# Threshold attention and GELU MLP on one core: order of the first loads, place and pace of the MLP, and a fifth pair with PE transposes

## The chip, the cores and the metric

The kernel runs on one core of a Trainium2 chip. The core has a matrix engine (TensorE, PE in the profile; PEld is its weight load), a vector engine (VectorE, DVE), an activation engine (ScalarE, ACT), GpSimd (POOL) and a queue engine (SyncE, SP). Each works through its own program in order, and they wait for each other on semaphores. The metric is the device time of one execution in microseconds (us), smaller is better; a kernel counts as faster or slower when its time differs by more than 2%.

## The reference

Attention on 8 batches of 8 heads (576 tokens, head size 64) in which only scores within `tau` of the row's maximum count, and after it an MLP with exact GELU on all 4608 tokens. The weights `w_in` and `w_out` come as 64-bit floats.

```python
# q, k, v: (8, 8, 576, 64) float32; tau = 0.02
scores = scale * np.matmul(q, k.transpose(0, 1, 3, 2))
thresh = np.max(scores, axis=-1, keepdims=True) - tau
scores = np.where(scores >= thresh, scores, -1000000000.0)
scores = scores - np.max(scores, axis=-1, keepdims=True)
attn = np.exp(scores)
attn = attn / (np.sum(attn, axis=-1, keepdims=True) + 1e-09)
attn_out = np.matmul(attn, v)
# bridge: (B,H,S,D) -> (B*S, H*D), x: (4608, 512)
h = x @ w_in                                   # (512, 2048)
g = 0.5 * h * (1.0 + erf(h * inv_sqrt2))
return g @ w_out                               # (2048, 512)
```

## The kernel before

The unit of attention is a pair of heads: 4 pairs in each batch, 32 in all. A pair has 5 slots: four of 128 query rows for both heads, and a last one for the 64 remaining rows of both heads. Slots of the first four pairs are walked in two sweeps, rows 0 to 255 of all four pairs first, so that a first block of x is there early. The MLP works on blocks of 256 tokens, 18 in all, and is laid between the slots in single steps.

At the start the loads are issued, and the first transposes:

```python
    load_early(0)
    for _ in range(4):
        load_piece()
    load_early(1)
    turn_qk_early(0)
    load_early(2)
```

A weight piece (512 columns of 128 rows) is loaded twice by GpSimd, once shifted by three bytes, and put together to 32-bit floats by three operations of VectorE, one of ScalarE and one more of VectorE:

```python
            piece = None
            if raws:
                dst, raw, shifted = raws.pop(0)
                hi = raw.rearrange("p (f w) -> p f w", w=2)[:, :, 1]
                top = shifted.rearrange("p (f w) -> p f w", w=2)[:, :, 0]
                expo, power = (gp.tile([P, PIECE], U32, tag="g", name=s) for s in ("expo", "power"))
                vec.tensor_scalar(expo, hi, 0x7FF00000, None, op0=ALU.bitwise_and)
                nc.scalar.activation(power, expo, AF.Relu, bias=rebias, scale=8.0)
                piece = dst, hi, top, power
                yield 340
            if ahead:
                dst, hi, top, power = ahead
                mant = gp.tile([P, PIECE], U32, tag="g", name="mant")
                vec.tensor_scalar(mant, top, 0x0FFFFFFF, 0x10000000, op0=ALU.bitwise_and, op1=ALU.bitwise_or)
                yield 340
                vec.scalar_tensor_tensor(power, hi, 0x80000000, power, op0=ALU.bitwise_and, op1=ALU.bitwise_or)
                yield 720
                vec.scalar_tensor_tensor(dst, mant, 2.0 ** -28, power.bitcast(FP32), op0=ALU.mult, op1=ALU.mult)
                load_piece()
                converted[0] += 1
                yield 700
            ahead = piece
```

The first four pairs ("early") turn q, k and the probabilities with PE, against the identity or a diagonal that holds the reciprocal of the row sum, so that the turn also scales. The others scale with VectorE, turn blocks of 32 x 32 with VectorE, and regroup them by DMA:

```python
    def softmax_tail(p, i, early):

        s = st[p]
        sc, thr, w = s.pop(("sc", i)), s.pop(("thr", i)), s["p", i]
        n = len(sc)
        den = small.tile([P, 2], FP32, tag="den", name="den")
        for e in range(n):
            row = w[:, e * S:(e + 1) * S].rearrange("p (h s) -> p h s", h=2)
            nc.vector.scalar_tensor_tensor(
                row, sc[e][:, :, 0:HALF], thr[:, e:e + 1], row, op0=ALU.is_ge, op1=ALU.mult,
                accum_out=den[:, e:e + 1])
        rden = small.tile([P, 2], FP32, tag="rden", name="rden")
        nc.vector.tensor_scalar(den[:, 0:n], den[:, 0:n], 1e-9, None, op0=ALU.add)
        nc.vector.reciprocal(rden[:, 0:n], den[:, 0:n])
        if early:
            diag = s["diag", i] = dg.tile([P, 2, P], FP32, tag="diag", name="diag")
            for e in range(n):
                nc.scalar.activation(diag[:, e, :], ident, AF.Copy, bias=0.0, scale=rden[:, e:e + 1])
            return
        for e in range(n):
            row = w[:, e * S:(e + 1) * S]
            nc.vector.tensor_scalar(row, row, rden[:, e:e + 1], None, op0=ALU.mult)

        s = st[p]
        w = s.pop(("p", i))
        n = 1 if i == NC else 2
        for e in range(n):
            to = pd_tail[p % 2] if i == NC else pd[e][:, :, i * Q:(i + 1) * Q]
            nc.vector.transpose(to[:, 0:NB, :], w[:, e * S:(e + 1) * S].rearrange("p (b i) -> p b i", i=Q))
        if i == NC - 1:
            s["pT"] = [one.tile([P, KR, S], FP32, tag=f"pT{e}", name=f"pT{e}") for e in range(2)]
            for e in range(2):
                for a in range(4):
                    regroup(s["pT"][e], a * P, P, pd[e], a)
        if i == NC:
            for a in range(4):
                e, at = divmod(a * Q, TAIL)
                regroup(s["pT"][e], MAIN + at, Q, pd_tail[p % 2], a)
# ...
    def turn_p_early(p, i):


        s = st[p]
        if i == 0 or (p < HP and i == 2):
            s["pT"] = [one.tile([P, KR, S], FP32, tag=f"pT{e}", name=f"pT{e}") for e in range(2)]
        w, diag = s.pop(("p", i)), s.pop(("diag", i))
        n = 1 if i == NC else 2

        def turn(to, cols, e):
            nc.tensor.matmul(to, lhsT=w[:, cols], rhs=diag[:, e, :], start=True, stop=True)

        for e in range(n):
            tr = ps.tile([P, NC, P], FP32, tag="mm", name="tr")
            for c in range(NC):
                at = e * (S + TAIL) + c * P
                turn(tr[:, c, :], slice(at, at + P), e)
            if i < NC:
                nc.scalar.copy(s["pT"][e][:, 0:NC, i * P:(i + 1) * P], tr)
```

The scores of a slot need two PSUM buffers of the tag `sc`, and there are two, so scores of the next slot wait until `softmax_tail` of this one has read them (L360).

The loop over slots, with the pace of the MLP:

```python
    BATCH = HP * SLOTS
    WEIGH = 2
    START = 2 * HP + 1

    goal = [0.55] + [1.85 + 2.06 * i for i in range(B - 1)]


    PART = (1.0, 1.2, 1.0, 1.0, 0.8)

    tokens = 0
    owed = 0.0
    for n in range(len(slots) + WEIGH + 1):
        p, i = slots[n] if n < len(slots) else divmod(n, SLOTS)
        batch = n // BATCH
        early = p < EARLY
        last = slots[n - 1] if 0 < n <= len(slots) else None
        if p < NP:
            scores(p, i)
            softmax_head(p, i)
        if last and last[0] < EARLY:
            turn_p_early(*last)
        if p < NP:
            softmax_tail(p, i, early)
            if not early and i:
                for c in range(0 if i == 1 else i, i + 1):
                    turn_p(p, c)
        if p < HP - 1 and i == 0:
            turn_qk_early(p + 1)
            if p == 0:
                load_early(3)
        if p < HP and i == NC and 0 < p < HP - 1:
            load(p + 3)
        if n == BATCH:
            convert(1e12)
            for t in pd_tail:
                nc.gpsimd.memset(t[:, NB:4 * KR, :], 0.0)
        if p >= HP and i == 1 and p + 2 < NP:
            load(p + 2)
        if p >= HP - 1 and i == 2 and p + 1 < NP:
            turn_qk(p + 1)
        convert(3000 if n < 2 * HP else 3600)
        if n >= START:
            done = min(batch, B - 1)
            rest = BATCH if done else BATCH - START
            part = PART[i] if not early and batch < B else 1.0
            owed += part * (goal[done] - (goal[done - 1] if done else 0.0)) * BLK_NS / rest
            if n % 2 or n >= EARLY * SLOTS:
                fill(owed, tokens)
                owed = 0.0
# ...
        if p > EARLY and i == WEIGH:
            for h in range(2):
                weigh_v(p - 1, h * HALF, (h + 1) * HALF)
            if p % HP == 0:
                tokens = p // HP * S
    convert(1e12)
    fill(1e12, B * S)
```

`goal` says how many blocks of the MLP should be issued by the end of each batch of 20 slots; `fill` issues steps until the debt is paid, and stops when the next block's x is not there (`tokens`) or its weights are not converted.

## Time and profile before

| | before |
|---|---|
| time, median of 3 (lowest, highest) | 1504.81 us (1501.78, 1504.85) |
| span of the profiled execution | 1498.2 us |
| mean granted clock of PE | 0.990 |
| matmuls of the MLP (L436, L447), busy | 516.7 + 515.7 us |
| matmuls of scores (L335) | 161.9 + 35.4 us |
| matmuls with v (L408) | 168.4 us |
| turns of early probabilities on PE (L281) | 47.4 us |
| weights moved by GpSimd's queue | 33.54 MB |

The profile page has a line of busy times for each engine, a strip of 40 equal slices of the span with the busy share in tenths, the DMA queues, the chain of work that ended last, and the costliest groups of instructions. A group's row gives line, engine and operation, what is written from what, the shape, the count, busy us and mean ns of one, and the idle time of the engine just before, with what ended it. Besides the page, the trace can be asked for waits, for a timeline, and for the busy time by windows. Times in a timeline row are start and length in us; square brackets hold the idle time before it and what released it.

### The profile page before, as it was taken

The numbers are of one execution on the slowest core, as the hardware profiler recorded it, in microseconds if no ns is written. First come the engines' busy times: TensorE is split into PE (matmuls) and PEld (weight loads), VectorE is DVE, ScalarE is ACT, GpSimd is POOL, SyncE is SP. The second block draws the span as 40 slices with busy tenths as digits, with TensorE's granted clock in tenths as the row PEclk, the third lists the DMA queues.
The fourth block names the chain that finished last, engine by engine and source line by source line (L and its number), as shares of the span: only waits on it lengthen the run. The fifth ranks groups of instructions, "written<-read, shape, count | busy, mean of one in ns | idle before, by whom it ended". The sixth has DMA issues, their size and how long they took to land.

```text
span 1498.2 us, 17694 instructions
## 1 busy us (share of the span) xinstructions
PE 1434.2 (96%) x6288; PEld 904.9 (60%) x6288; DVE 928.9 (62%) x2125; ACT 595.0 (40%) x886; POOL 41.2 (3%) x86
## 2 busy tenths in 40 slices
PE   3888899989999999989999999999999999999998
PEld 2566546546564747465656566666656565765764
DVE  3997788886667577766777677767767776100000
ACT  3657526535352525234444444444435352210110
POOL 2222100000000000000000000000000000000000
PEclk9999999999999999999999999999999999999999
DMA  7877336655555625463555554454544534300000
GB/s 230 245 242 239 109 76 128 115 121 105 103 104 106 117 64 101 95 135 64 110 106 111 99 111 98 105 98 98 103 95 97 106 73 94 79 14 8 7 14 14
DMA packets 390823, 155.05 MB, mean 103 GB/s; under 512 B 229456, under 2 KB 379984, under 8 KB 390736
## 3 DMA queue, kind: packets, MB, share of 16 engines
q1 hardware_dynamic: 383568, 120.38, 39.7%
q0 software_dynamic: 7168, 33.54, 6.5%
q8 instruction: 51, 0.84, 0.2%
q14 instruction: 36, 0.29, 0.1%
HBM read 61.85 MB, written 9.44 MB: 48 GB/s over the span
## 4 chain that ended last, share of the span: by engine, by line
PE 81%; DVE 11%; DMA 3%; SPq 2%; ACT 2%; issue 1%; DVEq 0%; ACTq 0%
PE o_ps L447 31%; PE hT L436 30%; PE sc L335 10%; PE xT L408 9%; DVE p L360 3%; DVE nmx L346 2%; SPq L397 2%; DMA pT<-pd 1%; DVE pd L385 1%; DMA q<-in_q_dram 1%; DVE power L176 1%; DVE expo L167 1%; DVE w_in L178 1%; PE tr L281 1%; ACT p L347 1%
## 5 line engine op out<-in xcount | busy, mean ns | idle before, releaser
L436 PE MATMUL hT<-x,w_in 128*128 128x256 f32 x2304 | 516.7, 382 | 0.7 <-ACT pT L289 0.7
L447 PE MATMUL o_ps<-w_out,g 128*128 128x512 f32 x1152 | 515.7, 598 | 0.0
L436 PEld LDWEIGHTS hT<-x,w_in 128*128 128x128 f32 x2304 | 433.1, 190 | 83.9 <-issue 26.1
L447 PEld LDWEIGHTS o_ps<-w_out,g 128*128 128x128 f32 x1152 | 214.4, 190 | 258.3 <-issue 254.7
L346 DVE TENSOR_REDUCE nmx<-sc 128x1 f32<-128x576 f32 x288 | 205.6, 751 | 258.5 <-PE sc L335 258.1
L347 ACT ACTIVATE p<-sc,nmx 128x576 f32<-128x576 f32 x288 | 203.4, 741 | 404.0 <-DVE nmx L346 403.5
L360 DVE SCALAR_TENSOR_TENSOR p<-sc,thr,p 128x576 f32<-128x576 f32 x288 | 225.3, 816 | 38.3 <-ACT p L347 25.5
L335 PE MATMUL sc<-kT,qT 64*128 64x288 f32 x960 | 161.9, 439 | 16.0 <-DVE p L360 15.6
L408 PE MATMUL xT<-pT,v 128*64 128x288 f32 (+2 forms) x1280 | 168.4, 415 | 7.5 <-issue 2.7
L385 DVE STREAM_TRANSPOSE pd<-p 128x576 f32<-128x576 f32 x224 | 157.6, 750 | 8.9 <-DMA pT<-pd 6.9
L335 PEld LDWEIGHTS sc<-kT,qT 64*128 64x128 f32 x960 | 90.0, 190 | 94.5 <-issue 77.6
L408 PEld LDWEIGHTS xT<-pT,v 128*64 128x64 f32 x1280 | 90.9, 139 | 85.2 <-issue 22.9
L440 ACT ACTIVATE g<-hT 128x512 f32<-128x512 f32 x144 | 85.3, 597 | 141.2 <-PE hT L436 140.4
L373 DVE TENSOR_SCALAR p<-p,rden 128x576 f32<-128x576 f32 x252 | 120.9, 518 | 4.9
L440 ACT ACT_TABLE_LOAD x71 | 91.1, 1283 | 12.7 <-PE hT L436 10.4
L347 ACT ACT_TABLE_LOAD x70 | 89.8, 1283 | 1.3
L417 ACT COPY x<-xT 128x256 f32<-128x256 f32 (+7 forms) x124 | 28.9, 287 | 143.8 <-PE xT L408 143.8
L450 ACT COPY o_sb<-o_ps 128x512 f32<-128x512 f32 x36 | 21.0, 584 | 142.0 <-PE o_ps L447 128.7
L281 PE MATMUL tr<-diag,p 128*128 128x128 f32 (+1 forms) x360 | 47.4, 296 | 6.3 <-ACT g L440 5.5
L281 PEld LDWEIGHTS tr<-diag,p 128*128 128x128 f32 (+1 forms) x360 | 40.3, 190 | 16.6 <-ACT g L440 6.4
L335 PE MATMUL sc<-kT,q_tail 128*128 128x288 f32 x120 | 35.4, 419 | 6.4 <-DVE p L360 6.4
L350 DVE TENSOR_SCALAR thr<-nmx,tau_eff 128x2 f32<-128x2 f32 (+1 forms) x160 | 36.1, 226 | 5.7
(68 smaller groups left out, 418.3 us busy)
## 6 DMA issues: line engine op xcount, KB each, us to landing
pT<-pd SPq DMA_DIRECT2D x224, 320.0 KB, 5.9
out_dram<-o_sb SPq DMA_DIRECT2D x36, 256.0 KB, 2.2
pT<-pd_tail SPq DMA_DIRECT2D x112, 80.0 KB, 2.9
q<-in_q_dram SPq DMA_DIRECT2D x112, 72.0 KB, 2.6
k<-in_k_dram SPq DMA_DIRECT2D x112, 72.0 KB, 2.8
v<-in_v_dram SPq DMA_DIRECT2D x168, 40.0 KB, 2.1
raw<-in_moe_w_in_dram POOLq DMA_DIRECT2D x8, 512.0 KB, 8.7
pd<-in_moe_w_in_dram POOLq DMA_DIRECT2D x8, 512.0 KB, 5.9
```

The lines of the kernel that those rows point to most:

```text
L281: nc.tensor.matmul(to, lhsT=w[:, cols], rhs=diag[:, e, :], start=True, stop=True)
L335: nc.tensor.matmul(sc[e][:, h, 0:HALF], lhsT=lhsT, rhs=s["kT"][rows, at:at + HALF], start=True, stop=True)
L346: nc.vector.tensor_reduce(nmx[:, e:e + 1], sc, axis=AXIS.XY, op=ALU.max, negate=True)
L347: nc.scalar.activation(w[:, e * S:(e + 1) * S].rearrange("p (h s) -> p h s", h=2), sc, AF.Exp, bias=nmx[:, e:e + 1], scale=1.0)
L350: nc.vector.tensor_scalar(thr[:, 0:n], nmx[:, 0:n], -1.0, tau_eff, op0=ALU.mult, op1=ALU.subtract)
L360: nc.vector.scalar_tensor_tensor(row, sc[e][:, :, 0:HALF], thr[:, e:e + 1], row, op0=ALU.is_ge, op1=ALU.mult, accum_out=den[:, e:e + 1])
L373: nc.vector.tensor_scalar(row, row, rden[:, e:e + 1], None, op0=ALU.mult)
L385: nc.vector.transpose(to[:, 0:NB, :], w[:, e * S:(e + 1) * S].rearrange("p (b i) -> p b i", i=Q))
L408: nc.tensor.matmul(xT[f, 0:hi - lo], lhsT=s["v"][:, e, c, :], rhs=pT[:, c, lo:hi], start=(c == 0), stop=(c == KR - 1))
L436: nc.tensor.matmul(hT[:, j % 2, :], lhsT=w_in_sb[c][:, j * P:(j + 1) * P], rhs=x_blk[n][:, c, :], start=(c == 0), stop=(c == N_DM - 1))
L440: nc.scalar.activation(t, hT, AF.Gelu)
L447: nc.tensor.matmul(o[:, 0:d_model], lhsT=g[j][:, m * P:(m + 1) * P], rhs=w_out_sb[j], start=(j == 0), stop=(j == N_DF - 1))
```

## The change

It has five parts.

- The q and k of pairs 0 and 1 are issued ahead of all weights, their k from ScalarE's queue; two weight pieces instead of four go out at the start, two more in slots 0 and 2; v follows later. This is to let slot 1 start without waiting for weights.
- `EARLY` is one larger: pair 4, the first of the second batch, is also turned by PE, when VectorE still finishes the weights.
- While pairs are early, the MLP's steps are put right behind the scores, ahead of the turns, and no longer at the end of the slot behind the weight conversions.
- For pairs 5 to 11, the first head of each slot is scaled by ScalarE, and the second by VectorE; the order of heads is reversed so that VectorE turns the second one meanwhile.
- The goal of the MLP is given at the slots where new x arrives, and lies just under the number of blocks whose x is there. The conversions are paced a little slower, and the flush of conversions at slot 20 is dropped.

```diff
@@ -54,7 +54,7 @@
     Q = 32
     HP = H // 2
     NP = B * HP
-    EARLY = HP
+    EARLY = HP + 1
     NC = S // P
     MAIN = NC * P
     TAIL = S - MAIN
@@ -222,16 +222,20 @@
         s = st[p] = {}
         for name, src in (("q", q), ("k", k)):
             t = s[name] = ld.tile([P, NC + 1, P], FP32, tag=name, name=name)
+            eng = nc.scalar if p < 2 and name == "k" else nc.sync
             for e in range(2):
-                nc.sync.dma_start(
+                eng.dma_start(
                     t[:, 0:NC, e * D:(e + 1) * D],
                     src[b, 2 * hp + e, 0:MAIN, :].rearrange("(t p) d -> p t d", p=P),
                 )
-            nc.sync.dma_start(
+            eng.dma_start(
                 t[0:TAIL, NC, :].rearrange("p (e d) -> p e d", e=2),
                 src[b, 2 * hp:2 * hp + 2, MAIN:S, :].rearrange("e s d -> s e d"),
             )
-        t = s["v"] = v_sb[p % 4]
+
+    def load_v_early(p):
+        b, hp = divmod(p, HP)
+        t = st[p]["v"] = v_sb[p % 4]
         for e in range(2):
             nc.sync.dma_start(t[:, e, 0:NC, :], v[b, 2 * hp + e, 0:MAIN, :].rearrange("(t p) d -> p t d", p=P))
             nc.sync.dma_start(t[e * TAIL:(e + 1) * TAIL, e, NC, :], v[b, 2 * hp + e, MAIN:S, :])
@@ -368,9 +372,12 @@
             for e in range(n):
                 nc.scalar.activation(diag[:, e, :], ident, AF.Copy, bias=0.0, scale=rden[:, e:e + 1])
             return
-        for e in range(n):
+        for e in reversed(range(n)):
             row = w[:, e * S:(e + 1) * S]
-            nc.vector.tensor_scalar(row, row, rden[:, e:e + 1], None, op0=ALU.mult)
+            if e == 0 and n == 2 and p < 3 * HP:
+                nc.scalar.activation(row, row, AF.Copy, bias=0.0, scale=rden[:, e:e + 1])
+            else:
+                nc.vector.tensor_scalar(row, row, rden[:, e:e + 1], None, op0=ALU.mult)
 
     def turn_p(p, i):
 
@@ -380,7 +387,7 @@
         s = st[p]
         w = s.pop(("p", i))
         n = 1 if i == NC else 2
-        for e in range(n):
+        for e in reversed(range(n)):
             to = pd_tail[p % 2] if i == NC else pd[e][:, :, i * Q:(i + 1) * Q]
             nc.vector.transpose(to[:, 0:NB, :], w[:, e * S:(e + 1) * S].rearrange("p (b i) -> p b i", i=Q))
         if i == NC - 1:
@@ -471,11 +478,13 @@
             mlp["next"] = next(mlp["steps"], None)
 
     load_early(0)
-    for _ in range(4):
+    load_early(1)
+    for _ in range(2):
         load_piece()
-    load_early(1)
     turn_qk_early(0)
+    load_v_early(0)
     load_early(2)
+    load_v_early(1)
 
     parts = [(range(2), HP), (range(2, SLOTS), HP)] + [(range(SLOTS), 1)] * (NP - HP)
     slots = []
@@ -486,7 +495,14 @@
     WEIGH = 2
     START = 2 * HP + 1
 
-    goal = [0.55] + [1.85 + 2.06 * i for i in range(B - 1)]
+    GOAL = [(-1, 0.0), (START - 1, 0.0), (BATCH - 1, 0.55)]
+    GOAL += [(BATCH * (m + 2) + WEIGH, x) for m, x in enumerate([1.96, 3.96, 5.96, 8.06, 10.16, 12.26, 14.36])]
+
+    def goal(n):
+        for (lo, x), (hi, y) in zip(GOAL, GOAL[1:]):
+            if lo <= n < hi:
+                return x + (y - x) * (n - lo) / (hi - lo)
+        return GOAL[-1][1]
 
 
     PART = (1.0, 1.2, 1.0, 1.0, 0.8)
@@ -501,6 +517,10 @@
         if p < NP:
             scores(p, i)
             softmax_head(p, i)
+        owed += (goal(n) - goal(n - 1)) * BLK_NS * (PART[i] if not early and p < NP else 1.0)
+        if early and n % 2:
+            fill(owed, tokens)
+            owed = 0.0
         if last and last[0] < EARLY:
             turn_p_early(*last)
         if p < NP:
@@ -512,25 +532,24 @@
             turn_qk_early(p + 1)
             if p == 0:
                 load_early(3)
+                load_v_early(2)
+                load_v_early(3)
+            if p < 2:
+                load_piece()
         if p < HP and i == NC and 0 < p < HP - 1:
-            load(p + 3)
+            if p + 3 < EARLY:
+                load_early(p + 3)
+                load_v_early(p + 3)
+            else:
+                load(p + 3)
         if n == BATCH:
-            convert(1e12)
             for t in pd_tail:
                 nc.gpsimd.memset(t[:, NB:4 * KR, :], 0.0)
         if p >= HP and i == 1 and p + 2 < NP:
             load(p + 2)
         if p >= HP - 1 and i == 2 and p + 1 < NP:
-            turn_qk(p + 1)
-        convert(3000 if n < 2 * HP else 3600)
-        if n >= START:
-            done = min(batch, B - 1)
-            rest = BATCH if done else BATCH - START
-            part = PART[i] if not early and batch < B else 1.0
-            owed += part * (goal[done] - (goal[done - 1] if done else 0.0)) * BLK_NS / rest
-            if n % 2 or n >= EARLY * SLOTS:
-                fill(owed, tokens)
-                owed = 0.0
+            (turn_qk if p + 1 >= EARLY else turn_qk_early)(p + 1)
+        convert(3000 if n < 2 * HP else 3400)
         if last and last[0] < EARLY:
             done, hp = divmod(last[0], HP)
             if last[1] == 1:
@@ -541,6 +560,9 @@
                 weigh_v(last[0], TOK, S)
                 if hp == HP - 1:
                     tokens = (done + 1) * S
+        if not early:
+            fill(owed, tokens)
+            owed = 0.0
         if p > EARLY and i == WEIGH:
             for h in range(2):
                 weigh_v(p - 1, h * HALF, (h + 1) * HALF)
```

## The prediction

> **What bounds the kernel now.** I read the shares of busy time first, then the same by stages, then what TensorE (PE) waited for, then the timeline at the longest waits. The page's busy lines:
>
> ```profile
> PE 1434.2 (96%) x6288; PEld 904.9 (60%) x6288; DVE 928.9 (62%) x2125; ACT 595.0 (40%) x886; POOL 41.2 (3%) x86
> ...
> PE   3888899989999999989999999999999999999998
> ```
>
> PE is busy for 1434.2 of 1498.2 us, so a change that removes no matmul can win at most the 64 us of idle, plus what matmuls lose while the array is slow. The digits put the idle at the front. So I cut the span at the starts of slots in the timeline of the score matmuls: slot 1 at 27, slot 20 (pair 4 begins) at 178, slot 42 (first x of the second batch is finished) at 320, the last visible hole at 660, the end of attention at 1283. Columns: window, its length, then busy us of PE, PEld, DVE, ACT, POOL, granted clock, DMA share, GB/s.
>
> ```profile
> 0.00:27.00 27.00, 7.19 (x26) 4.88 (x26) 5.16 (x18) 5.34 (x8) 9.46 (x26) 1.00 0.84 260
> 27.00:178.00 151.00, 128.62 (x785) 93.55 (x784) 131.03 (x315) 97.44 (x181) 31.42 (x59) 0.95 0.71 218
> 178.00:320.00 142.00, 133.21 (x560) 74.39 (x559) 120.70 (x278) 62.23 (x88) 0.31 (x1) 0.99 0.51 101
> 320.00:660.00 340.00, 330.71 (x1454) 205.66 (x1455) 241.11 (x545) 135.39 (x197) 0.00 (x0) 0.98 0.51 103
> 660.00:1283.00 623.00, 623.00 (x2727) 390.56 (x2726) 430.88 (x974) 271.84 (x375) 0.00 (x0) 1.00 0.49 99
> ```
>
> PE idle is 19.8, 22.4, 8.8, 9.3 and 0 us. Between 27 and 178 VectorE (DVE) is as full as PE (131.0 against 128.6 of 151), because it converts the weights there. From 660 on nothing but PE counts. What PE waits for, in the table of waits over the whole run (us, times, longest):
>
> ```profile
> PE sc L335 <- DVE p L360: 23.6, 18, 3.1
> ...
> PE tr L255 <- DMA q<-in_q_dram: 18.5, 2, 14.0
> ...
> PE tr L281 <- ACT g L440: 5.5, 2, 4.1
> ```
>
> The 14.0 is one wait, in the timeline of PE at the start:
>
> ```profile
> 8.38 2.57 PE L335 MATMUL sc<-kT,qT 64*128 64x288 f32 x8 [0.27 <-ACT kT L260]
> 24.96 1.08 PE L255 MATMUL tr<-ident,q 128*128 128x128 f32 x4 [14.01 <-DMA q<-in_q_dram]
> ```
>
> Pair 1's q was queued behind four pieces of weights (eight transfers of 512 KB); slot 1's scores stand behind its transposes in PE's program. The 4.1 is in the timeline at 164 us: the Gelu was written after two weight conversions on ScalarE (ACT), and PE's transposes of p wanted the PSUM that it frees:
>
> ```profile
> 163.64 1.09 ACT L440 ACTIVATE g<-hT 128x512 f32<-128x512 f32 x2
> ...
> 164.29 4.41 PE L281 MATMUL tr<-diag,p 128*128 128x128 f32 x20 [4.13 <-ACT g L440]
> ```
>
> Of the 23.6 us, some 7 come where the MLP has run out of x, just before a batch ends; the timeline of PE near 645 us:
>
> ```profile
> 640.48 1.94 PE L335 MATMUL sc<-kT,qT 64*128 64x288 f32 x8 [1.74 <-DVE p L360]
> 645.13 2.99 PE L335 MATMUL sc<-kT,qT 64*128 64x288 f32 x8 [2.71 <-DVE p L360]
> 648.05 6.07 PE L408 MATMUL xT<-pT,v 128*64 128x288 f32 x40
> 654.06 1.24 PE L335 MATMUL sc<-kT,qT 64*128 64x288 f32 x8
> ```
>
> No MLP matmul stands between the scores, and eight score matmuls take 2.99 us instead of 1.24.
>
> **What the Trainium skill says.** "TensorE: Matmul & The Clock Gate", section "Why this matters for your kernels", warns of idle gaps beyond about 3 us: the array falls back to half clock. The trace leans that way with even shorter gaps: 2.99 against 1.24 us above, and a granted clock of 0.95 in the second stage. So an avoided hole is worth more than its length. "DMA: Bandwidth & Descriptors", section "Issuing engines are not separate DMA queues": transfers issued by different engines interleave on the same 16 DMA engines, and a second issuer saves only issue time. The trace agrees: pair 1's q, issued by SyncE from 8.3 us, landed at 24.8 while GpSimd's weights were moving. So k on ACT's queue gains about 2 us of issue; the order of issue is what counts. "ScalarE: Activation LUTs", section "Table sets: the hidden batching unit", puts copy into every table set: scaling a head with Copy should load no table. The trace has 71 loads in front of Gelu and 70 in front of Exp, of 1283 ns each, and one at the first activation; none before the Copy lines otherwise.
>
> **The change part by part.**
>
> *q and k of pairs 0 and 1 ahead of the weights.* SyncE took 3.6 us to issue pair 0's six q and k transfers (1.18 to 4.78). With k on ACT, q and k of both pairs are issued in about that time, just before GpSimd starts the weights at 4.63. That is 1.18 MB (576 x 64 x 4 B x 2 heads x 2 tensors x 2 pairs); at the 260 GB/s of the first window it is there by about 8 us, before slot 0's scores end at 10.95. Pair 1's transposes then run at about 11 to 13, and slot 1's scores wait only for the score PSUM, which slot 0's L360 frees at 14.0 as before: 14 instead of 27.0, 13 us gained. Against that: DVE's first conversions now come at about 15 us, and need 2.5 pieces (2.6 MB) by 18; behind 1.2 MB of q and k at 260 GB/s they land at about 15 to 20. I take off 1.5. Net -11.5.
>
> *MLP right behind the scores.* Gelu now stands ahead of the copies, the diagonal and the conversions in ACT's program. It removes the 5.5 us of L281 behind Gelu and part of the 7.6 us that scores wait in this stage (Exp then seldom waits for a Gelu). But a slot with MLP delays ACT's "power" step and so DVE's conversions; DVE is the co-bound. Two small reliefs for DVE: a convert debt of 3400 instead of 3600 in 12 slots pushes one piece (0.42 + 0.42 + 0.69 + 0.69 = 2.2 us) past slot 20, and pair 4's q and k are turned by PE (0.74 + 0.67 + 0.45 us off DVE). I take -4 of the 22.4.
>
> *Pair 4 early.* PE gets a quarter of the early L281 work: (39.7 + 9.0) / 4 = 12.2 us in the stage 178 to 320, and 1.8 us of L255/L263, the latter in slot 17 where DVE sets the pace. DVE loses nine transposes of 0.75 and nine scalings of 0.518, 11.4 us; ACT gets eight copies of 0.59, four of 0.29 and nine diagonals of 0.395, 9.4 us. DVE was busy 120.7 of 142, so the relief alone buys little; it takes waits away.
>
> *One head scaled by ACT, pairs 5 to 11.* 28 times 0.518 = 14.5 us off DVE, 28 times about 0.74 (the Exp of the same shape takes 0.741) = 21 us onto ACT, which is busy only 62 of 142. In this stage a late pair costs DVE about 31 us, 6.2 a slot; 2.1 less makes 5.8, about what PE has in a slot. So I expect most of the 8.8 us of waits for L360 to go (-6), and with them the slow scores (26.0/145 = 0.179 us each against 0.155 later, and 5.9/16 against 5.7/20 for the tails: together 5 us; -3 of it). The stage: +12.2 - 6 - 3 = +3.
>
> *Pace.* MLP progress was meant to be 2.16 blocks at slot 42, where only 2 are possible (576 tokens), 4.22 of 4 at slot 62, 6.28 of 6 at slot 82. The new goal is 1.96, 3.96 and 5.96. The holes at 318, 480 and 640 should close: 9.3 us of idle in the stage 320 to 660, and its slow matmuls (46.8 - 272 x 0.155 = 4.6 for scores, 48.3 - 360 x 0.127 = 2.6 for L408). I take -12 of 16.5. From 660 on, 0: the same matmuls, with PE already full.
>
> Sum: -11.5 - 4 + 3 - 12 = -24.5. Span 1498.2 - 24.5 = 1474; the timed median lies 6.6 us above the span, so about 1480 us.
>
> **Rivals.** (a) *The extra PE work eats it.* PE is 96% busy and gets 14 us more. If the holes in the second to fourth stage close only half, the sum is -11.5 - 2 + 7.5 - 6 = -12: 1493. For it: at slot 20 to 25 PE had no long holes. (b) *The start only moves the wait.* Weights land later, DVE waits for them, and since DVE fills 131 of 151 us, everything up to slot 20 follows. The DMA share was 0.84 in the start; against it, GpSimd waited 100 us for DVE to free buffers, so the transfers have slack later. It would leave 6 of 11.5: 1486. (c) *ACT becomes the tight engine in early slots*: Gelu ahead of the copies holds up diagonals, copies and "power" in order, and DVE starves; ACT was busy 97 of 151 there. It costs 5 to 10 us: 1485 to 1490. (d) *Everything closes*: also the 22.4 us of the second stage to under 10, giving 1467.
>
> **Range and chances.** Rivals (a) to (c) lie 5 to 13 us above the sum and partly add; (d) 13 below. I take 1467 to 1496. Two per cent faster is 1474.7, 5 us under my middle: 0.32. Slower by 2% (1534.9) would need a new stall of 55 us: 0.03.
>
> **What would show it.** Slot 1's scores start at 14 to 16 us and the wait of L255 for q is a few us; slot 20 starts at about 163; L281's wait for Gelu is gone; x450 of L281 with about 60 us busy; slot 42 at about 308; no idle of PE over 1 us from 320 to 660; ACT rows on the scaling line, x28, near 0.74 us, with no table loads of their own. Wrong would be: L255 still waiting 8 us or more, DVE waiting for raw weights, or L335 waiting for L360 as long as before.

## The result and the profile after

The changed kernel takes 1493.55 us (median of 4, 1491.38 to 1498.07) against 1504.83 us: a ratio of 0.9934, 95% interval 0.9908 to 0.996. The gain of 11 us is clear of noise, but it is 0.7%, under the 2% that counts as faster, and 25 us were forecast. A second measurement of the same kernel on the chip of later runs gave 1495.3 us, ratio 0.9947 (0.993 to 0.9965).

The page of the changed kernel: busy times, and the strip of PE.

```profile
span 1496.3 us, 17938 instructions
...
PE 1451.5 (97%) x6388; PEld 921.7 (62%) x6388; DVE 908.4 (61%) x2083; ACT 644.2 (43%) x952; POOL 40.5 (3%) x86
...
PE   7889898999999999999999999999999999999998
```

PE is busy 17.3 us more than before (1434.2), and idle 44.8 us instead of 64.0. The profiled execution is one at the upper end of this kernel's times and that of before at the lower end of its own, so the spans differ by 1.9 us only. The same windows as in the prediction, for the changed kernel:

```profile
0.00:27.00 27.00, 16.72 (x69) 12.44 (x70) 15.49 (x44) 11.71 (x20) 11.25 (x30) 0.95 0.99 278
27.00:178.00 151.00, 130.71 (x782) 95.66 (x783) 122.26 (x297) 94.48 (x173) 28.59 (x55) 0.93 0.70 215
178.00:320.00 142.00, 132.82 (x593) 79.87 (x589) 99.73 (x232) 74.30 (x114) 0.62 (x2) 0.96 0.36 70
320.00:660.00 340.00, 338.83 (x1495) 209.09 (x1494) 244.29 (x551) 169.66 (x233) 0.00 (x0) 1.00 0.54 107
```

The first and the last row are as hoped: 9.5 us more work done by 27 us, and 338.8 of 340 us busy up to 660. The two in the middle are not. PE is busy there 2.1 us more in one and 0.4 us less in the other than before, and the granted clock is lower (0.93 and 0.96 against 0.95 and 0.99). The waits of PE over the whole run:

```profile
PE sc L339 <- DVE p L364: 17.3, 15, 2.3
PE tr L259 <- DMA q<-in_q_dram: 6.5, 1, 6.5
PE xT L415 <- issue: 4.7, 2, 2.6
PE xT L415 <- DVE pT L296: 3.6, 4, 2.5
PE tr L259 <- DMA k<-in_k_dram: 3.0, 1, 3.0
PE xT L415 <- DVE q_tail L272: 2.5, 1, 2.5
```

The 14.0 us behind pair 1's q and the 5.5 behind Gelu are gone. In their place stand small waits of the v matmuls for VectorE (L296, L272). The timeline of PE at the start:

```profile
12.50 1.06 PE L259 MATMUL tr<-ident,k 128*128 128x128 f32 x4
15.64 0.34 PE L267 MATMUL tr<-ident,q 64*128 64x64 f32 x1 [2.08 <-DMA q<-in_q_dram]
...
15.88 2.26 PE L339 MATMUL sc<-kT,qT 64*128 64x288 f32 x8
```

Slot 1's scores start at 15.9 instead of 27.0. And at the place of the hole at 645 us, the timeline of PE now has MLP between the scores:

```profile
638.76 1.24 PE L339 MATMUL sc<-kT,qT 64*128 64x288 f32 x8
639.93 6.28 PE L454 MATMUL o_ps<-w_out,g 128*128 128x512 f32 x14
646.14 5.07 PE L415 MATMUL xT<-pT,v 128*64 128x288 f32 x40
651.14 1.24 PE L339 MATMUL sc<-kT,qT 64*128 64x288 f32 x8
```

In the kernel before, the eight score matmuls that took 2.99 us there, behind a hole of 2.71 us, ran at a granted clock of 0.50 (third number from the end of its window row); from 638 to 656 us the changed kernel has 1.00 throughout.

```profile
645.10:648.10 3.00, 2.97 (x10) 1.86 (x10) 2.90 (x8) 0.00 (x0) 0.00 (x0) 0.50 0.69 131
```

Where the time went shows best by slots. Each slot has one instruction that makes its threshold (L350 before, L354 after) in VectorE's timeline; its start marks the slot. Lengths of the stretches between such marks in us, for the profiled execution of each run (the runs are explained below):

| run | to slot 1 | 1 to 20 | 20 to 26 | 26 to 42 | 42 to 82 | 82 to end |
|---|---|---|---|---|---|---|
| before | 33.4 | 147.6 | 39.2 | 107.4 | 323.5 | 847.1 |
| changed | 22.0 | 153.8 | 50.1 | 109.1 | 306.4 | 854.8 |
| changed, again | 21.5 | 153.6 | 50.1 | 109.4 | 306.4 | 854.9 |
| e9 loads alone | 21.9 | 151.4 | 38.8 | 107.7 | 325.7 | 847.7 |
| e10 goal alone | 34.5 | 146.8 | 38.8 | 108.3 | 306.9 | 854.7 |
| e11 loads and goal | 21.7 | 146.3 | 38.8 | 108.6 | 306.4 | 854.7 |
| e12 = e11 + pair 4 | 21.2 | 149.2 | 49.7 | 105.1 | 305.4 | 854.8 |
| e13 = e11 + scaling on ACT | 21.1 | 147.9 | 37.7 | 113.8 | 308.1 | 854.7 |
| e14 = e11 + place of the MLP | 21.1 | 150.6 | 38.8 | 107.4 | 305.4 | 854.7 |
| e15 = e11 + heads reversed | 21.1 | 149.2 | 40.4 | 110.0 | 305.3 | 854.7 |
| e16 = e11 + pace of conversions | 21.3 | 148.0 | 38.8 | 106.9 | 306.8 | 854.7 |

The changed kernel wins 11.4 us up to slot 1, and 9.4 from slot 42 to the end (the last stretch is longer mostly because the new goal leaves a tenth of a block more for it: 5.9 blocks are issued by slot 82, and 6 before). It gives back 6.2 from slot 1 to 20 and 12.6 from slot 20 to 42. The stretch from 1 to 20 scatters: runs with the same program up to slot 20 have 147.4 (e4, below), 151.3 (e2), 153.6 and 153.8, so a few us there prove nothing. The scatter goes with the granted clock. Here is the stretch in the changed kernel and in e4; the same 782 matmuls keep PE busy for 132.8 us at 0.92 and for 127.4 at 0.96:

```profile
22.02:175.84 153.82, 132.81 (x782) 96.86 (x782) 124.88 (x301) 97.02 (x180) 30.38 (x58) 0.92 0.72 217
```

```profile
21.14:168.52 147.38, 127.40 (x782) 93.72 (x782) 124.78 (x301) 96.49 (x180) 30.37 (x58) 0.96 0.75 229
```

Most of the 6.2 us given back there can therefore be clock. The two traces of the changed kernel agree within 0.5 us in every stretch.

### The profile page after: what moved, and what is told of

Its sections match the earlier page's. It is cut to its first block, busy times and chain, and to the rows that moved or that the text cites. A ratio compares the mean times of both kernels' runs of the same rounds, so it can differ in the third digit from the quotient of the medians.

```text
span 1496.3 us, 17938 instructions
## 1 busy us (share of the span) xinstructions
PE 1451.5 (97%) x6388; PEld 921.7 (62%) x6388; DVE 908.4 (61%) x2083; ACT 644.2 (43%) x952; POOL 40.5 (3%) x86
## 4 chain that ended last, share of the span: by engine, by line
PE 87%; DVE 6%; DMA 3%; ACT 2%; SPq 2%; issue 1%; DVEq 0%; ACTq 0%
PE o_ps L454 32%; PE hT L443 32%; PE sc L339 11%; PE xT L415 10%; DVE p L364 2%; SPq L404 2%; DVE nmx L350 2%; PE tr L285 1%; DVE pd L392 1%; DMA q<-in_q_dram 1%; DMA k<-in_k_dram 1%; ACT p L351 0%; DMA pT<-pd 0%; ACT L351 0%; DVE power L176 0%
## 5 line engine op out<-in xcount | busy, mean ns | idle before, releaser
L443 PE MATMUL hT<-x,w_in 128*128 128x256 f32 x2304 | 524.2, 385 | 0.0
L350 DVE TENSOR_REDUCE nmx<-sc 128x1 f32<-128x576 f32 x288 | 205.7, 751 | 250.1 <-PE sc L339 249.8
L364 DVE SCALAR_TENSOR_TENSOR p<-sc,thr,p 128x576 f32<-128x576 f32 x288 | 225.3, 816 | 56.8 <-ACT p L351 44.8
L415 PE MATMUL xT<-pT,v 128*64 128x288 f32 (+2 forms) x1280 | 171.0, 418 | 11.1 <-issue 4.7
L392 DVE STREAM_TRANSPOSE pd<-p 128x576 f32<-128x576 f32 x216 | 151.7, 750 | 5.8 <-DMA pT<-pd 5.2
L380 DVE TENSOR_SCALAR p<-p,rden 128x576 f32<-128x576 f32 x215 | 104.6, 518 | 4.7
L351 ACT ACT_TABLE_LOAD x78 | 100.1, 1283 | 13.4 <-DVE nmx L350 12.2
L447 ACT ACT_TABLE_LOAD x79 | 101.4, 1283 | 9.4 <-PE hT L443 8.0
L285 PE MATMUL tr<-diag,p 128*128 128x128 f32 (+1 forms) x450 | 57.2, 290 | 0.0
L285 PEld LDWEIGHTS tr<-diag,p 128*128 128x128 f32 (+1 forms) x450 | 50.2, 187 | 11.2 <-issue 4.1
L378 ACT ACTIVATE p<-p,rden 128x576 f32<-128x576 f32 x28 | 21.7, 776 | 42.7 <-DVE rden L369 42.7
L339 PE MATMUL sc<-kT,q_tail 128*128 128x288 f32 x120 | 34.5, 410 | 5.5 <-DVE p L364 5.4
```

The lines of the kernel that those rows point to most:

```text
L339: nc.tensor.matmul(sc[e][:, h, 0:HALF], lhsT=lhsT, rhs=s["kT"][rows, at:at + HALF], start=True, stop=True)
L350: nc.vector.tensor_reduce(nmx[:, e:e + 1], sc, axis=AXIS.XY, op=ALU.max, negate=True)
L351: nc.scalar.activation(w[:, e * S:(e + 1) * S].rearrange("p (h s) -> p h s", h=2), sc, AF.Exp, bias=nmx[:, e:e + 1], scale=1.0)
L364: nc.vector.scalar_tensor_tensor(row, sc[e][:, :, 0:HALF], thr[:, e:e + 1], row, op0=ALU.is_ge, op1=ALU.mult, accum_out=den[:, e:e + 1])
L415: nc.tensor.matmul(xT[f, 0:hi - lo], lhsT=s["v"][:, e, c, :], rhs=pT[:, c, lo:hi], start=(c == 0), stop=(c == KR - 1))
L443: nc.tensor.matmul(hT[:, j % 2, :], lhsT=w_in_sb[c][:, j * P:(j + 1) * P], rhs=x_blk[n][:, c, :], start=(c == 0), stop=(c == N_DM - 1))
```

## The experiments

Sixteen runs, in the order of the argument. Medians are of 4 to 6 executions; ratios are to the kernel before on the same chip. e10, e15, e16 and e18 were measured on another chip than e11, so differences between runs are taken from the ratios. No run is 2% faster or slower than the kernel before.

| run | median us | ratio | 95% interval |
|---|---|---|---|
| changed, again | 1495.3 | 0.9947 | 0.993 to 0.9965 |
| e1 pair 4 late again | 1490.7 | 0.9920 | 0.9907 to 0.9933 |
| e2 VectorE scales again | 1492.5 | 0.9928 | 0.9916 to 0.9941 |
| e3 MLP last again | 1492.37 | 0.9931 | 0.9918 to 0.9944 |
| e4 old goal | 1507.15 | 1.0031 | 1.0017 to 1.0046 |
| e8 copies later | 1499.7 | 0.9981 | 0.9967 to 0.9994 |
| e9 loads alone | 1493.86 | 0.9936 | 0.9918 to 0.9953 |
| e10 goal alone | 1490.62 | 0.9929 | 0.9912 to 0.9945 |
| e11 loads and goal | 1478.23 | 0.9839 | 0.9824 to 0.9854 |
| e7 changed less the three parts | 1484.9 | 0.9877 | 0.9862 to 0.9892 |
| e12 e11 + pair 4 | 1488.07 | 0.9903 | 0.9886 to 0.9919 |
| e13 e11 + scaling on ACT | 1484.7 | 0.9874 | 0.986 to 0.9889 |
| e14 e11 + place | 1480.35 | 0.9855 | 0.9835 to 0.9875 |
| e15 e11 + heads reversed | 1482.45 | 0.9864 | 0.9847 to 0.9881 |
| e16 e11 + conversions | 1475.57 | 0.9826 | 0.9811 to 0.9841 |
| e18 e11 + scaling, other order | 1481.61 | 0.9862 | 0.9849 to 0.9876 |

### One part undone at a time (e1 to e4)

e1, pair 4 with VectorE's turns again:

```diff
-    EARLY = HP + 1
+    EARLY = HP
```

> The changed kernel with pair 4 turned by VectorE and DMA again (EARLY = HP), all else kept. Theory T1 (the turns of pair 4 on TensorE are paid in full, 12 us between slots 20 and 26, and VectorE's relief is worth nothing because VectorE has slack there): the time falls by 8 to 13 us against the changed kernel (1493.5), to about 1481 to 1485, and slots 20 to 26 take about 39 us again instead of 57. Rival R1 (without the early pair VectorE becomes the bound in slots 20 to 26, with the last conversions in them): within 3 us of 1493.5, with the waits of the scores for L364 growing by some 10 us.

It came out at 1490.7: R1 by the time, T1 by the first slots. (PE's waits for L364 from slot 20 to 42 grew from 8.5 to 11.0 us, not by the 10 of R1.) Slots 20 to 26 took 40.4 us, as T1 says, but slots 26 to 42 took 115.5, 6.4 more, of which most goes with v matmuls that now stand behind slot 26 (152 there instead of 106, 6.3 us more of busy time). The sum of the two, 155.9, is only 3.3 under the changed kernel and 9.3 over the kernel before, which has no early pair 4 either. Something else in the changed kernel costs time there.

e2, both heads scaled by VectorE:

```diff
-            if e == 0 and n == 2 and p < 3 * HP:
+            if False:
```

> The changed kernel with both heads scaled by VectorE in pairs 5 to 11. Theory T2 (the relief of VectorE is lost because ScalarE does the scaling ahead of the next Exp, and the scores still wait for L364): within 3 us of 1493.5; VectorE's waits for Exp between slots 20 and 42 fall from 12 us to some 4, and its busy time grows by 14.5 us. Rival R2 (the scaling by ScalarE does hold the waits down): 4 to 8 us slower than 1493.5, with the idle of TensorE between slots 26 and 42 growing by that much.

1492.5, as T2 had it; between slots 20 and 42 VectorE's wait for Exp fell from 12.0 to 2.2 us. But its wait for the regroup transfers rose from 4.1 to 11.8, which e15 takes up below.

e3, the MLP of early slots at the end of the slot:

```diff
-        if early and n % 2:
-            fill(owed, tokens)
-            owed = 0.0
         if last and last[0] < EARLY:
             turn_p_early(*last)
# ...
         convert(3000 if n < 2 * HP else 3400)
+        if early and n % 2:
+            fill(owed, tokens)
+            owed = 0.0
```

> The changed kernel with the MLP of early slots at the end of the slot again, behind the conversions. Prediction's step (the place right behind the scores saves some 4 us between slots 8 and 20): 3 to 6 us slower than 1493.5, and the wait of TensorE's turns for a Gelu is back with about 5 us. Rival R3 (the same time is lost elsewhere, since VectorE is the bound there): within 2 us of 1493.5.

1492.37: R3. No gain from the place can be seen. The timeline of the changed kernel at slots 16 and 17 shows what took the place of the wait for Gelu:

```profile
140.90 7.36 PE L443 MATMUL hT<-x,w_in 128*128 128x256 f32 x26
...
148.09 1.42 PE L285 MATMUL tr<-diag,p 128*128 128x128 f32 x10
149.18 0.76 DVE L296 COPY pT<-tr 128x256 f32<-128x256 f32 x2 [4.43 <-PE tr L285]
...
150.32 0.82 DVE L364 SCALAR_TENSOR_TENSOR p<-sc,thr,p 128x576 f32<-128x576 f32 x1
...
153.39 4.60 PE L415 MATMUL xT<-pT,v 128*64 128x320 f32 x20 [2.46 <-DVE q_tail L272]
```

The turns now stand behind 7.4 us of MLP. VectorE's copies out of the turns of a last slot stand ahead of the masking (L364) in its program, so VectorE waits 4.4 us for PE, and then PE waits 2.5 for VectorE.

e4, the old goal:

```diff
-    GOAL = [(-1, 0.0), (START - 1, 0.0), (BATCH - 1, 0.55)]
-    GOAL += [(BATCH * (m + 2) + WEIGH, x) for m, x in enumerate([1.96, 3.96, 5.96, 8.06, 10.16, 12.26, 14.36])]
+    POINTS = [0.55] + [1.85 + 2.06 * i for i in range(B - 1)]
# ... goal(n) is linear within each batch of 20 slots
```

> The changed kernel with the old goal of MLP progress (0.55, then 1.85 + 2.06 per batch). Prediction's step (the old goal runs out of x just before slots 42, 62 and 82): 8 to 12 us slower than 1493.5, with idle of TensorE of about 9 us between 320 and 660 us. Rival R4 (what is not issued there is issued later at the same cost, since the sum of matmuls is the same): within 3 us.

1507.15, by the ratios 13 to 15 us slower than the changed kernel, and slower than before. With the old goal, PE is busy 9.3 us less in the window of the holes (338.83 above):

```profile
320.00:660.00 340.00, 329.57 (x1431) 203.33 (x1429) 230.39 (x519) 144.91 (x211) 0.00 (x0) 0.98 0.52 104
```

So without the goal nothing is left of the changed kernel's gain, and the load order's 11 us are lost to something that no single undoing brought back. That calls for building up from the kernel before.

### A repair that failed (the changed kernel again, e8)

> The changed kernel once more, for a second trace and a second median on the same chip as the runs below. All theories: 1491 to 1495 us; the stretch from slot 1 to slot 20 between 147 and 152 us instead of the 153.8 of the first trace, if that was the scatter of the granted clock.

1495.3, with 153.6 us from slot 1 to 20: the same stretches as in the first trace. (That the stretch scatters with the clock is shown by e4 and e2 instead.)

e8 puts the copies of L296, and the small ones of L308 after them, behind the masking; `turn_p_early` hands them back to be called later:

```diff
-        if last and last[0] < EARLY:
-            turn_p_early(*last)
+        copies = turn_p_early(*last) if last and last[0] < EARLY else None
         if p < NP:
             softmax_tail(p, i, early)
+            if copies:
+                copies()
```

> The changed kernel with VectorE's copies out of the turns of a pair's last slot put behind the masking of the next slot (they stood in front of it, and waited up to 4.4 us for TensorE's turns behind the MLP). Theory T4 (this wait of VectorE, 6 to 7.6 us in two slots, is why the MLP right behind the scores gained nothing): 3 to 6 us faster than the changed kernel, 1488 to 1490. Rival R7 (TensorE is the bound in these slots): within 2 us of it.

1499.7, by the ratios 5 us slower than the changed kernel on the same chip. VectorE's wait for the turns fell from 7.6 to 1.8 us up to slot 26, but PE's v matmuls now wait for the copies, in the table of waits between slots 1 and 26:

```profile
PE xT L419 <- DVE pT L307: 11.0, 4, 4.5
```

The copies stand in the way of both engines; moving them turned one wait into the other. Both T4 and R7 miss: the order matters, but in the other direction.

### The loads and the goal alone (e9, e10, e11)

e9 is the kernel before with the new order of first loads, e10 with the new goal, e11 with both. The edits are those parts of the change's diff.

> The kernel before with only the order of the first loads changed (q and k of pairs 0 and 1 first, their k from ScalarE's queue, two weight pieces at the start). Prediction's step: slot 1 starts 11 to 12 us earlier and the whole run is 10 to 12 us faster than before, about 1491 to 1493. Rival R5 (VectorE and the x that is there set the pace up to slot 42, so an earlier start is given back as waiting): gain under 5 us, the stretch from slot 1 to slot 42 longer by 6 us or more.

> The kernel before with the new goal alone. Prediction's step: 10 to 12 us faster than before, 1491 to 1493; together with the 9 us of the loads alone this would not reach the 25 us of both. If the gains add up to what both brought: 14 to 16 us faster, about 1488.

> The kernel before with the new order of loads and the new goal, without the early pair 4, without scaling on ScalarE, MLP of early slots at the end of the slot. Theory T3 (these two carry the whole gain, and the other three parts together cost as much as either brings): about 1480 us, range 1477 to 1484. Rival R6 (the new start and the new goal overlap, because the thinner pace up to slot 42 lets the granted clock fall): 1487 to 1493, with slow matmuls of over 10 us between slots 26 and 42 as in the changed kernel (5.6 before).

e9 gained 9.6 us (ratio 0.9936), e10 10.7 (0.9929), e11 24.2 (0.9839): the steps of the prediction at about their size, and within the intervals they add up. T3 holds: the rest of the change costs more than either part brings. In e11 the stretch from 20 to 42 is 147.4 us, as before (146.6), so neither an earlier start nor the thinner pace harms it, and R6 falls. (As a measure of slow matmuls, take their busy time between slots 26 and 42, less their count times their mean busy time from 660 to 1283 us in the kernel before. It is 5.7 us before and in e9, about 8 with the new goal, in e10 and e11, and 10.9 in the changed kernel.) Which piece of the new order brings the 9.6 us, the order itself, ScalarE's queue or the later v, was not separated.

### What the other parts cost (e12 to e16, e7, e18)

e12 adds the early pair 4 to e11 (`EARLY = HP + 1`, with the loads and turns that follow from it).

> Loads and goal on the kernel before, plus pair 4 turned by TensorE. Theory T1 (13 us more TensorE work between slots 20 and 42 are paid nearly in full, because VectorE is not what bounds these slots): 10 to 13 us over 1478.2, so 1488 to 1491, with slots 20 to 26 some 11 us longer and slots 26 to 42 as long as without it. Rival R1 (VectorE's relief pays for it, and only the scaling on ScalarE did the harm): 1478 to 1483.

1488.07, ratio 0.0064 or 9.6 us worse than e11: T1. The busy times from slot 20 to slot 42, first e11, then e12:

```profile
167.90:315.30 147.40, 134.13 (x554) 74.74 (x556) 124.87 (x287) 60.60 (x86) 0.31 (x1) 0.98 0.53 105
```

```profile
170.40:325.20 154.80, 144.39 (x652) 84.62 (x654) 115.86 (x272) 68.34 (x107) 0.62 (x2) 0.99 0.41 81
```

PE is busy 10.3 us more, VectorE 9.0 less, and the stretch is 7.4 longer: slots 20 to 26 10.9 longer, slots 26 to 42 3.5 shorter. The group row of L285 in e12's window has 90 turns in 11.1 us of busy time. VectorE's relief became waiting for scores (22.7 us in e12, 4.9 in e11).

e13 adds the scaling on ScalarE to e11, as the change has it.

> Loads and goal on the kernel before, plus one head scaled by ScalarE in pairs 4 to 11. Theory T5 (the scaling in front of the next Exp in ScalarE's program delays the Exp, and with it the scores' buffers, by more than it relieves VectorE): 5 to 9 us over 1478.2, so 1483 to 1487; VectorE's waits for Exp between slots 20 and 42 rise from about 2 to 12 us. Rival R2 (harmless alone, VectorE's 14 us of relief outweigh it): 1475 to 1479.

1484.7, 5.3 us worse than e11 by the ratios: the time of T5. As the change has it, this part also reverses the heads, which e15 below measures alone. Two timelines of slot 31, ScalarE and VectorE. First e11:

```profile
235.25 0.82 DVE L364 SCALAR_TENSOR_TENSOR p<-sc,thr,p 128x576 f32<-128x576 f32 x1
...
236.97 0.60 ACT L444 ACTIVATE g<-hT 128x512 f32<-128x512 f32 x1
...
237.58 1.28 ACT L351 ACT_TABLE_LOAD   x1
...
238.11 1.42 DVE L350 TENSOR_REDUCE nmx<-sc 128x1 f32<-128x576 f32 x2
238.90 1.41 ACT L351 ACTIVATE p<-sc,nmx 128x576 f32<-128x576 f32 x2
...
239.89 0.82 DVE L364 SCALAR_TENSOR_TENSOR p<-sc,thr,p 128x576 f32<-128x576 f32 x1
```

Then e13:

```profile
238.14 0.82 DVE L364 SCALAR_TENSOR_TENSOR p<-sc,thr,p 128x576 f32<-128x576 f32 x1 [1.22 <-ACT p L351]
...
240.14 0.78 ACT L378 ACTIVATE p<-p,rden 128x576 f32<-128x576 f32 x1 [1.40 <-DVE rden L369]
...
240.93 1.28 ACT L447 ACT_TABLE_LOAD   x1
...
241.49 1.42 DVE L350 TENSOR_REDUCE nmx<-sc 128x1 f32<-128x576 f32 x2 [0.83 <-PE sc L339]
242.23 0.60 ACT L447 ACTIVATE g<-hT 128x512 f32<-128x512 f32 x1
242.84 1.28 ACT L351 ACT_TABLE_LOAD   x1
...
244.14 1.37 ACT L351 ACTIVATE p<-sc,nmx 128x576 f32<-128x576 f32 x2
244.91 0.82 DVE L364 SCALAR_TENSOR_TENSOR p<-sc,thr,p 128x576 f32<-128x576 f32 x1 [1.74 <-ACT p L351]
```

In e11 ScalarE has loaded Gelu's table, run Gelu and loaded Exp's again by the time the row maximum is there: Exp starts 0.79 us after the reduction does. In e13 the scaling first waits 1.40 us for the reciprocal and runs 0.78; the two table loads of 1.28 us and Gelu are queued behind it, and Exp starts 2.65 us after the reduction. From masking to masking this slot takes 6.8 instead of 4.6 us; most differ less, and the 16 slots from 26 to 42 together take 5.2 us more. VectorE's wait for Exp from slot 20 to 42 is 13.9 us in e13 and 2.2 in e11. Its busy time is 7.0 us less, and none of it is won.

There is a second delay, which the queue of slot 31 does not show. In e11 the load of Exp's table starts right behind what ScalarE did before, ahead of the row maximum. In e13 it waits for the maximum in some slots. The group rows of these loads from slot 20 to 42, first e11, then e13 (after the second bar, the idle time in front of them):

```profile
L351 ACT ACT_TABLE_LOAD x8 | 10.3, 1283 | 0.1
```

```profile
L351 ACT ACT_TABLE_LOAD x8 | 10.3, 1283 | 4.6 <-DVE nmx L350 4.5
```

In the trace of e13, six of the eight loads have a separate wait for VectorE in front of them, and the Exp behind waits for a semaphore of ScalarE itself; in e11 no load has one, and Exp alone waits, for VectorE. So where ScalarE also writes p by scaling, Exp waits for two engines, one of the waits comes ahead of the load, and 1.28 us of loading can no longer be done while the maximum is computed. That it is the write of p which adds the wait fits e15, where VectorE scales and no load has one.

e18 was meant to mend this: ScalarE scales head 1, heads stay in order, and the MLP of late slots (with its Gelu) is issued ahead of the scaling.

```diff
+        if not early:
+            owed += (goal(n) - goal(n - 1)) * BLK_NS * (PART[i] if p < NP else 1.0)
+            fill(owed, tokens)
+            owed = 0.0
         if last and last[0] < EARLY:
             turn_p_early(*last)
# ...
+            if e == 1 and p < 3 * HP:
+                nc.scalar.activation(row, row, AF.Copy, bias=0.0, scale=rden[:, e:e + 1])
```

> Loads and goal on the kernel before, plus one head scaled by ScalarE in pairs 4 to 11, but so that the two suspected harms are gone: ScalarE takes head 1 and the natural order stays, and the MLP of late slots is issued ahead of the scaling, so that Gelu and its table load no longer stand behind the scaling and before the next Exp. Theory T7 (the relief of VectorE is worth something once the order is right): 2 to 6 us below 1478.2, VectorE's waits for Exp back at 2 to 5 us between slots 26 and 42. Rival R10 (VectorE's relief is worth nothing in these slots, whatever the order): 1477 to 1482.

1481.61, still 3.5 us worse than e11 by the ratios, with intervals that overlap at the edge; the wait for Exp remained at 10.8 us from slot 20 to 42. The new order took Gelu out from between the scaling and Exp, but not the separate wait in front of the load: six of eight loads have it again. Slot 30, and the group row of the loads:

```profile
235.26 1.52 DVE L350 TENSOR_REDUCE nmx<-sc 128x1 f32<-128x576 f32 x2
...
236.06 1.28 ACT L351 ACT_TABLE_LOAD   x1 [1.43 <-DVE nmx L350]
...
237.35 1.37 ACT L351 ACTIVATE p<-sc,nmx 128x576 f32<-128x576 f32 x2
```

```profile
L351 ACT ACT_TABLE_LOAD x8 | 10.3, 1283 | 10.9 <-DVE nmx L350 10.9
```

R10 fits the time, but the test of T7 is not clean, because the delay of Exp was not taken away. Whether VectorE's relief would be worth something without it stays open. What e18 does show is that scaling on ScalarE costs time with the heads in order too.

e14 adds the place of the MLP to e11.

> Loads and goal on the kernel before, plus the MLP of early slots right behind the scores. Prediction's step: 3 to 5 us faster than 1478.2, 1473 to 1475, the wait of the turns for a Gelu gone. Rival R3 (VectorE then waits for the turns behind the MLP as long as TensorE waited before): within 2 us of 1478.2.

1480.35; the intervals of e14 and e11 overlap. R3: the turns' wait for Gelu (4.1 us in e11) is gone, VectorE's wait for the turns is there with 6.6 us, and the turns wait 2.9 us for a copy of x.

e7 is the changed kernel with these three parts undone. It differs from e11 by the reversed heads, the pace of conversions and, at slot 20 alone, the MLP behind the v matmuls.

> The changed kernel without the early pair 4, without scaling on ScalarE and with the MLP of early slots at the end of the slot; it keeps the slower pace of conversions (3400, no flush) and the reversed order of heads. Theory T3 (the three parts cost the difference to the run with loads and goal alone): 1477 to 1481 us. Rival R8 (the small parts that are left, pace of conversions and order of heads, carry some of the cost): 1483 or more.

1484.9, so R8: 5.7 us by the ratios are left over. e15 and e16 add one of the small parts each to e11:

```diff
# e15
-        for e in range(n):
+        for e in reversed(range(n)):      # scaling and turning
# e16
-            convert(1e12)                 # at slot 20
-        convert(3000 if n < 2 * HP else 3600)
+        convert(3000 if n < 2 * HP else 3400)
```

> Loads and goal on the kernel before, plus the reversed order of the two heads in scaling and turning on VectorE, nothing else. Theory T6 (the regroup transfers of head 1 are issued after those of head 0, so turning head 1 first makes VectorE wait for them): 4 to 7 us over 1478.2, 1482 to 1485, VectorE's wait for the regroup transfers between slots 26 and 42 about 17 us as in the run with the three parts undone (7 with the natural order). Rival R9 (the slower conversions are what that run lost by): within 2 us of 1478.2.

> Loads and goal on the kernel before, plus the slower pace of conversions (3400 instead of 3600, no flush at slot 20). Theory T6: within 2 us of 1478.2. Rival R9: 1483 or more.

e15: 1482.45, 3.8 us worse than e11 by the ratios, with intervals that overlap at the edge (0.9847 and 0.9854). e16: 1475.57, 2.0 us better, with overlapping intervals. So R9 falls, and of the two the reversed order is the one that costs time. But together they make 1.8 us of the 5.7 that e7 lies above e11; the other 3.9 are within what the intervals allow, and if they are real, they come from neither part alone, and the cause stays open. VectorE's wait for the regroup transfers from slot 20 to 42, in e11, e15 and e7:

```profile
DVE pd L389 <- DMA pT<-pd: 7.1, 3, 3.0
```

```profile
DVE pd L389 <- DMA pT<-pd: 11.3, 3, 4.2
```

```profile
DVE pd L392 <- DMA pT<-pd: 17.3, 4, 4.7
```

e15's 11.3 us are less than the 17 expected, and its stretch is 3.0 us longer than e11's. Head 0's regroup is issued first and head 1's last; with the heads reversed, the next pair's first turn writes head 1's buffer. That fits the rows; a swap of the issue order, which would prove it, was not tried.

The parts measured on e11, by ratios: pair 4 +9.6, scaling with the reversed order that it came with +5.3, place +2.4, conversions -2.0; together +15.3. The changed kernel lies 0.0095 to 0.0108 of the ratio, 14 to 16 us, above e11. The sum fits, though each part is uncertain by about 3 us, and e7 shows that the parts need not simply add.

Within e13's 5.3 us, scaling and order are not separated: e13 lies 1.5 us above e15, less than the intervals can tell apart. Each costs time without the other, 3.5 us in e18 and 3.8 in e15.

The fastest of the versions measured is e16: the kernel before with the new order of loads, the new goal and the slower conversions. 1475.57 us, ratio 0.9826, ahead of both kernels; its interval overlaps e11's.

## Why the prediction was wrong

The time, 1493.55, lies inside the range of 1467 to 1496, but the gain was 11 us where the sum had 24.5. Step by step:

- *q and k ahead: right.* Net -11.5 expected; 11.4 us by slot 1, and 9.6 alone. But slot 20 was to come some 15 us earlier and slot 42 at about 308 instead of 320; by the marks slot 20 came 5.2 us earlier and slot 42 7.5 later. The first transposes started at 6.5 instead of 4.5 us, with twice the loads in flight, and the conversions at 17.2, some 2 us later than supposed. Slot 1's scores at 15.9 were inside the 14 to 16.
- *MLP right behind the scores: wrong.* "I take -4 of the 22.4." The wait for Gelu went, as said, but VectorE's copies of the turns took its place; e14 (+2.4 us, within the intervals) and e3 show no gain. The prediction saw the risk only for the "power" step.
- *Pair 4 early: the cost a little high, what was set against it wrong.* +12.2 us of L281; the busy time of L285 rose by 9.8 over the run, and pair 4 alone cost 9.6 us. VectorE's relief took no wait away: its waits for scores from slot 20 to 42 rose from 4.9 to 22.7 us (e12).
- *One head scaled by ACT: the step that failed.* "So I expect most of the 8.8 us of waits for L360 to go (-6), and with them the slow scores [...] -3 of it. The stage: +12.2 - 6 - 3 = +3." The stage, slot 20 to 42, came out 12.6 us longer, about what pair 4 alone was to cost. With this part alone on e11 (e13) the stage is 4.1 us longer, where 9 shorter were expected, and the run 5.3. L364's waits stayed at 8.5 us, and the slow matmuls between slots 26 and 42 grew from 5.7 to 10.9. The step took VectorE's busy time for what sets the slot. In the timelines of slot 31 it is a chain over three engines that sets it (scores, maximum, Exp, masking, scores again), and the scaling was put into its ScalarE link: Exp came later, behind the scaling, Gelu and two table loads in some slots, behind a table load that waited for the maximum in others, and VectorE's wait for Exp rose from 2.2 to 13.9 us (e13). The prediction counted 21 us onto an engine that is busy 62 of 142 and stopped there. What it took from the Trainium skill ("ScalarE: Activation LUTs", section "Table sets: the hidden batching unit": copy is in every table set) holds: L378 has no table load of its own and takes 0.776 us. The loads rose from 70 and 71 to 78 and 79, but e11, without the scaling, has as many, so that is the new goal. It read no part of the change into the reversed heads, 3.8 us by themselves (e15), which are part of the 5.3.
- *Pace: right.* -12 expected; -9.4 from slot 42 on, -10.7 alone, 13 to 15 lost when undone.

Of the rivals, (a) was nearest, at 1493, with the right reason for half of it: the extra PE work is paid in full. (c) named ScalarE, but for the early slots and for Gelu, not for the scaling. More than 2%, which was given a chance of 0.32, was reached by no version: e11 gained 1.6%, e16 1.7%.

## What to carry to other kernels

Neither relief of VectorE, 9.0 us in e12 and 7.0 in e13, shortened the stretch it was taken from: busy time alone did not tell what a slot waits for. Before moving an instruction to an engine with idle time, look in the timeline at what is queued behind it there, and at which waits it adds to the next instructions: here a table load of 1.28 us that had been hidden came to stand behind such a wait. Set a pace by the data that is there at each moment: a goal of 2.16 blocks where 2 exist left holes and slow matmuls behind them, and one just under 2, 4 and 6 was worth 11 us. When a change of several parts gains less than its best part, build up from the kernel before, part by part; here, undoing the three losing parts one at a time gave at most 4 us each, and hid a loss of 15.

## What had not been expected

The order in which two heads are turned costs 3.8 us (e15), probably through buffers whose transfers are issued one after the other. Scaling on ScalarE put a wait in front of the load of Exp's table. The start and the pace together brought 24.2 us, against 9.6 + 10.7 alone, a difference within the intervals. And e11's executions agree better than the changed kernel's: 1477.2 to 1479.7 against 1491.1 to 1498.3; the granted clock from slot 1 to 20, 0.98 in e11's trace and 0.92 in both of the changed kernel's, may be part of it, but why it differs is not known.
